# Fewer groups of narrow matmuls in a token-and-channel mixer: hidden product and last query transposes in one PSUM bank, stores at other ticks, second weights through ScalarE

## The chip, the cores and the metric

The kernel runs on one core of one Trainium2 chip. The metric is the device time in microseconds (us) of one execution; the median of three runs stands for a kernel. The engines are named as the profile names them: PE (TensorE matmul) with its weight loads PEld, DVE (VectorE), ACT (ScalarE), POOL (GpSimd) and SP (SyncE, which here only issues transfers).

## The reference, cut to what matters

```
q, k, v: (8 batches, 8 heads, 576 tokens, 64)
q_s = exp(q - max_d q) / (sum_d + 1e-9)            # over the head dimension
k_s = exp(k - max_s k) / (sum_s + 1e-9)            # over the tokens
x   = q_s @ (k_s^T @ v)                            # linear attention, then (8, 576, 512)
u   = x + (relu(x^T @ w_tok1) @ w_tok2)^T          # token mixing, 576 -> 256 -> 576
y   = u + relu(u @ w_ch1) @ w_ch2                  # channel mixing, 512 -> 1536 -> 512
z   = layernorm(y) * g_ln
out = y + relu(z @ w2_ch1) @ w2_ch2                # second channel mixing, 512 -> 2048 -> 512
```

The four channel and two token weights arrive as 64-bit floats and are turned into 32-bit ones on the chip.

## The kernel before

Every product is split into three: each operand is kept as a high and a low part (`hi`, `lo`), and `PASSES` runs hi*hi, hi*lo and lo*hi into the same PSUM bank. So each large product is made of matmuls of 128x128 weights with 512 columns ("wide" below), and PE has little else to do.

There are three stretches. From 0 to about 130 us the first 8 of 32 attention units run alone with the loads of the first weights. One unit is one batch and two heads (class `Unit`). Then come nine blocks of 512 tokens of the first channel mixing (`Phase1`, j = 0 to 8; block 0 is cut in two around block 1, and block 8 is made of the 64 last tokens of each batch), each of 12 steps f. While blocks 0 and 2 to 6 run, the other 24 units run between their wide matmuls, four to a block. From about 868 us on there are nine blocks of the second channel mixing (`Phase2`), 16 steps each.

The order is written out by hand (`tc.manual_schedule`). A clock of ticks moves on in the middle and at the end of each step's two products (`L1`, `L2`), so in `Phase1` one tick is six wide matmuls and a block has 48 ticks; in `Phase2` a tick is a whole product of 12. `later(n, fn)` puts a piece of work n ticks ahead. The units of a block start 10 ticks apart, and `Unit.start` gives each of a unit's pieces its tick (`when`). So the pieces of two units interleave. In a unit's own ticks: 2 transpose of the key maxima (`k_top`, tile pt), 4 its broadcast (`k_sub`, pb), 8 keys times values (pk), 10 the first token product (`tok1`, pg), 11 four query transposes (`q_T(0)`, pq), 12 the fifth (`q_T(1)`, pq), 13 the hidden layer of the token mixing (`hidden`, ph, two fp32 matmuls which the trace shows as four), 15 and 16 the two halves of the second token product (`tok2`, pu). Tick 12 of a unit is tick 2 of the next.

All these narrow pieces take their PSUM bank from one pool of two banks (`ps_att`), in turn: a piece must wait until the piece two before it has been read out. Reading out is a copy of the high part on ACT and a subtraction on DVE for the low part (`split`, `relu_split`).

When a `Phase1` block ends (`finish`, two steps into the next block), DVE adds the residual into yT, POOL adds its low part over all of yT, and four `y_store` pieces follow at ticks 5, 7, 9 and 11 from there: four transposes on PE (py), a copy on ACT and a transfer to `y_dram`.

The weights of the second channel mixing are turned into 32-bit parts in 32 chunks during `Phase1` blocks 7 and 8 and `Phase2` block 0 (class `Loads`, function `decode` with `late` true): a transfer of 512 KB into one of two buffers st, four DVE instructions, a DVE cast for the high part and a POOL subtraction for the low part. `Loads` was given depth 1, so one chunk is fetched ahead. Loads, and the reads of y for the layer norm (`load_y`), all go through SP's queue in program order. `Norm` makes the layer norm of a block: load, statistics, scaling (`hat`), and four groups of transposes (`turn`, px).

Of the kernel before, what the change touches and what calls it, by code (L numbers as in the profile page):

```python
# [16 lines left out]
P = 128  # L17
# [7 lines left out]
def kernel(  # L25
# [61 lines left out]
    def decode(st, w, hi, lo):  # L87
# [38 lines left out]
        def parts():  # L126
            x = w((box["t"] if late else w0).bitcast(F32))
            if late:
                vec.tensor_copy(out=hi, in_=x)  # L129
                nc.gpsimd.tensor_tensor(out=lo, in0=x, in1=hi.bitcast(F32), op=ALU.subtract)  # L130
            else:
                split(x, hi, lo, nc.gpsimd)
# [268 lines left out]
    class Unit:  # L401
# [7 lines left out]
        def start(self, at):  # L409
            steps = (  # L410
                self.k_max, self.k_top, self.q_max, self.q_sub, self.k_sub, self.q_exp,
                self.q_norm, self.k_exp, self.q_split, self.kv, self.tok1,
                lambda: self.q_T(0), self.hidden, lambda: self.q_T(1),
                lambda: self.tok2(0), lambda: self.tok2(1),
            )
            if self.n == 0:
                later(at + 10, lambda: loads.until(3))
                later(at + 14, lambda: loads.until(len(tok)))
            if self.early:
                when = (0, 1, 1, 1, 3, 3, 4, 5, 7, 8, 10, 10, 11, 12, 14, 15)  # L420
            else:
                when = (0, 2, 1, 2, 4, 4, 5, 6, 8, 8, 10, 11, 13, 12, 15, 16)
            for n, fn in zip(when, steps):
                later(at + n, fn)
# [120 lines left out]
        def q_T(self, i):  # L545
# [5 lines left out]
            if not self.early:  # L551
                pq = psum("pq")
                for c in range(c0, c1):
                    m = (c - c0) * P
                    nc.tensor.transpose(out=pq[:, m:m + P], in_=self.qt[:, c], identity=ident)
                split(pq[:, 0:n], self.qT[:, 0, sl], self.qT[:, 1, sl], nc.vector)
# [17 lines left out]
        def hidden(self):  # L574
            ph = psum("ph", self.early)
# [71 lines left out]
    class Phase1:  # L647
# [51 lines left out]
        def finish(self):  # L699
# [14 lines left out]
            if self.f0 == 0:  # L714
                nc.gpsimd.tensor_tensor(out=yT, in0=yT, in1=u[:, 1].bitcast(F32), op=ALU.add)  # L715
            for c in range(CT):
                later(5 + 2 * c, lambda c=c: y_store(self.j, c))
# [10 lines left out]
    class Norm:  # L728
# [3 lines left out]
        def start(self, at):  # L732
# [9 lines left out]
            for kk in range(KD):  # L742
                later(at + 12 + kk + kk // 2, call(self.turn, kk))
# [102 lines left out]
    with tc.manual_schedule():  # L846
# [89 lines left out]
        for o, f in steps:  # L936
            if isinstance(o, Phase1):
# [4 lines left out]
                if f == 0:  # L942
# [3 lines left out]
                    elif o.j == B - 1:  # L946
# [4 lines left out]
                        extra.clear()  # L951
# [6 lines left out]
                        ], 1, 1, 8)  # L958
                        for n in range(5, 29):
                            later(n, lambda: loads.pump(2))  # L960
                        later(10, load_ends)
                    elif o.j == NB - 1:
                        Norm(0).start(18)
# [53 lines left out]
```

## Time and profile before

| | |
|---|---|
| median of 3 runs | 1693.29 us (1693.03 to 1695.51) |
| profiled execution | 1692.61 us, of which the span in the trace is 1690.8 us |
| busy share of the span | PE 98%, PEld 82%, DVE 39%, ACT 23%, POOL 19% |
| wide matmuls | 6048 of PE's 8136 matmuls, 128x512 |
| granted TensorE clock | 0.998 of full speed over the span |

The page's first part gives busy time by engine, its fourth the chain that ended last, followed back from the end; its fifth the groups of instructions. In the timeline view a row is a run of like instructions: start in us from the span's start, length, engine, line, operation, tile written and tiles read, shape and count. Matmuls overlap their neighbours, so the length of a run says less than the distance from its start to the start of the next run; the text below works with these distances.

### The profile page before, as it was taken

The numbers are of one execution on the slowest core, as the hardware profiler recorded it, in microseconds if no ns is written. First come the engines' busy times: TensorE is split into PE (matmuls) and PEld (weight loads), VectorE is DVE, ScalarE is ACT, GpSimd is POOL, SyncE is SP. The second block draws the span as 40 slices with busy tenths as digits, with TensorE's granted clock in tenths as the row PEclk, the third lists the DMA queues.
The fourth block names the chain that finished last, engine by engine and source line by source line (L and its number), as shares of the span: only waits on it lengthen the run. The fifth ranks groups of instructions, "written<-read, shape, count | busy, mean of one in ns | idle before, by whom it ended". The sixth has DMA issues, their size and how long they took to land.

```text
span 1690.8 us, 20156 instructions
## 1 busy us (share of the span) xinstructions
PE 1650.4 (98%) x8136; PEld 1379.6 (82%) x8136; DVE 665.7 (39%) x1322; ACT 393.8 (23%) x792; POOL 314.2 (19%) x220
## 2 busy tenths in 40 slices
PE   5999999999999999999999899999999999999998
PEld 4888888888888888888788788888888888888887
DVE  6875434343433434354567722222213122222211
ACT  4663323333232323311211111111111111111110
POOL 5744522232222313221222200000000000000000
PEclk9999999999999999999999999999999999999999
DMA  8452312122121212042225310101010102010010
GB/s 228 124 169 67 98 33 74 43 56 50 38 67 30 71 38 74 21 144 63 88 63 174 100 51 25 50 25 50 25 51 25 50 1 75 1 53 23 0 50 25
DMA packets 122062, 105.39 MB, mean 62 GB/s; under 512 B 92976, under 2 KB 101424, under 8 KB 118512
## 3 DMA queue, kind: packets, MB, share of 16 engines
q1 hardware_dynamic: 115568, 86.27, 17.6%
q10 hardware_dynamic: 5248, 9.44, 1.6%
q0 software_dynamic: 1152, 8.39, 1.2%
q8 instruction: 64, 1.05, 0.3%
q14 instruction: 30, 0.25, 0.0%
HBM read 82.05 MB, written 22.02 MB: 62 GB/s over the span
## 4 chain that ended last, share of the span: by engine, by line
PE 57%; DVE 3%; DMA 1%; POOL 0%; issue 0%; ACT 0%; SPq 0%; ACTq 0%; DVEq 0%
PE ph L814 22%; PE acc L829 22%; PE acc L692 5%; PE ph L675 5%; PE px L789 1%; DMA st<-in_moe_w_ch 1%; PE pu L592 1%; PE py L622 0%; PE pg L538 0%; DVE t L115 0%; DVE t L121 0%; POOL yT L715 0%; DVE t L108 0%; DMA y<-y_dram 0%; DVE y L778 0%; DMA y_dram<-yn 0%
## 5 line engine op out<-in xcount | busy, mean ns | idle before, releaser
L142 DVE SCALAR_TENSOR_TENSOR h<-ph,h 128x512 fp32r<-128x512 f32 x252 | 174.1, 691 | 687.9 <-ACT h L141 687.8
L814 PE MATMUL ph<-xT,w 128*128 128x512 f32 x1728 | 420.9, 392 | 2.3 <-DVE h L142 1.0
L829 PE MATMUL acc<-w,h 128*128 128x512 f32 x1728 | 420.0, 392 | 0.0
L814 PEld LDWEIGHTS ph<-xT,w 128*128 128x128 f32 x1728 | 322.8, 188 | 73.8 <-DVE h L142 1.6
L829 PEld LDWEIGHTS acc<-w,h 128*128 128x128 f32 x1728 | 323.0, 188 | 68.8
L141 ACT ACTIVATE h<-ph 128x512 fp32r<-128x512 f32 x252 | 150.8, 598 | 858.7 <-PE ph L814 636.3
L692 PE MATMUL acc<-h,w 128*128 128x512 f32 x1296 | 328.7, 396 | 0.0
L675 PE MATMUL ph<-u,w 128*128 128x512 f32 x1296 | 327.7, 396 | 0.0
L675 PEld LDWEIGHTS ph<-u,w 128*128 128x128 f32 x1296 | 236.2, 189 | 46.9 <-DVE u L612 0.4
L692 PEld LDWEIGHTS acc<-h,w 128*128 128x128 f32 x1296 | 236.2, 188 | 45.6
L844 POOL DMA_DIRECT2D out<-y x8 | 4.5, 558 | 637.4 <-DVE y L840 637.4
L467 POOL TENSOR_TENSOR qt<-rawq,qm 128x640 f32<-128x640 f32 x24 | 30.3, 1262 | 235.0 <-PE pt L461 153.7
L538 PE MATMUL pg<-w,qn 128*128 128x256 f32 x480 | 64.8, 286 | 6.4 <-ACT w L137 3.4
L538 PEld LDWEIGHTS pg<-w,qn 128*128 128x128 f32 x480 | 62.2, 193 | 9.8 <-POOL qn L138 3.9
L130 POOL TENSOR_TENSOR w<-t,w 128x512 fp32r<-128x512 f32 x32 | 42.9, 1341 | 130.8 <-DVE w L129 126.3
L592 PE MATMUL pu<-w,hs 128*128 128x288 f32 x384 | 61.4, 295 | 0.0
L592 PEld LDWEIGHTS pu<-w,hs 128*128 128x128 f32 x384 | 54.4, 188 | 0.3 <-ACT hs L141 0.2
L715 POOL TENSOR_TENSOR yT<-yT,u 128x2048 f32<-128x2048 f32 x8 | 37.2, 4648 | 69.8 <-DVE yT L713 65.6
L138 DVE TENSOR_TENSOR qT<-pq,qT 128x512 fp32r<-128x512 f32 (+1 forms) x48 | 21.8, 454 | 71.3 <-ACT qT L137 71.3
L482 POOL TENSOR_TENSOR kt<-rawk,kb 128x640 f32<-128x640 f32 x24 | 37.8, 1575 | 50.2 <-ACT kb L478 50.2
L138 POOL TENSOR_TENSOR qn<-qt,qn 128x640 fp32r<-128x640 f32 x24 | 38.2, 1591 | 41.7 <-ACT qn L137 41.7
L138 DVE TENSOR_TENSOR u<-pu,u 128x288 fp32r<-128x288 f32 x32 | 14.6, 455 | 67.8 <-ACT u L137 67.7
(132 smaller groups left out, 1256.3 us busy)
## 6 DMA issues: line engine op xcount, KB each, us to landing
st<-in_moe_w_ch SPq DMA_DIRECT2D x41, 512.0 KB, 3.7
y<-y_dram SPq DMA_DIRECT2D x18, 1024.0 KB, 4.8
vt<-in_v SPq DMA_DIRECT2D x64, 128.0 KB, 2.9
y_dram<-yn ACTq DMA_DIRECT2D x32, 256.0 KB, 2.4
out<-y POOLq DMA_DIRECT2D x8, 1024.0 KB, 4.1
rawk<-in_k SPq DMA_DIRECT2D x54, 128.0 KB, 2.7
rawq<-in_q SPq DMA_DIRECT2D x27, 256.0 KB, 3.0
stages<-in_moe_w_ch SPq DMA_DIRECT2D x9, 512.0 KB, 4.5
```

The lines of the kernel that those rows point to most:

```text
L130: nc.gpsimd.tensor_tensor(out=lo, in0=x, in1=hi.bitcast(F32), op=ALU.subtract)
L138: engine.tensor_tensor(out=lo, in0=x, in1=hi.bitcast(F32), op=ALU.subtract)
L141: nc.scalar.activation(out=hi, in_=x, func=AF.Relu)
L142: nc.vector.scalar_tensor_tensor(out=lo, in0=x, scalar=0.0, in1=hi.bitcast(F32), op0=ALU.max, op1=ALU.subtract)
L482: nc.gpsimd.tensor_tensor(out=self.kt, in0=self.kr, in1=kb.to_broadcast([P, NC + 1, 2, D]), op=ALU.subtract,)
L538: nc.tensor.matmul(out=pg[:, 0:T], lhsT=self.qn[:, x, c], rhs=w1[:, y, c, :], start=(n == 0), stop=(n == len(terms) - 1),)
L592: nc.tensor.matmul(out=pu[:, 0:HN], lhsT=l, rhs=r, start=(n == 0), stop=(n == len(terms) - 1))
L675: nc.tensor.matmul(out=ps, lhsT=w[:, x, kk, fo:fo + P], rhs=u[:, y, kk], start=(n == 0), stop=(n == 3 * KD - 1),)
L692: nc.tensor.matmul(out=self.acc[dd], lhsT=w[:, x, f % 2, dd * P:(dd + 1) * P], rhs=h[:, y], start=(f == self.f0 and n == 0), stop=(f == se ...
L715: nc.gpsimd.tensor_tensor(out=yT, in0=yT, in1=u[:, 1].bitcast(F32), op=ALU.add)
L814: nc.tensor.matmul(out=ps, lhsT=w[:, x, kk, fo:fo + P], rhs=xT[:, y, kk], start=(n == 0), stop=(n == 3 * KD - 1),)
L829: nc.tensor.matmul(out=self.acc[c], lhsT=h[:, x, c * P:(c + 1) * P], rhs=w[:, y, f % 2], start=(f == 0 and n == 0), stop=(f == self.f1 - 1 ...
```

## The change

It has five parts.

- `hidden` of the 24 late units is moved from tick 13 to tick 12 and into the bank of the fifth query transpose: `q_T(1)` puts its transpose behind column 256 and `hidden` fills columns 0 to 255 of the same tile pq.
- The four stores of blocks 0 to 6 come at ticks 5, 8, 12 and 15 after the block's end (before: 5, 7, 9, 11).
- POOL's addition into yT is cut into four quarters (one per store), two ticks apart from block 2 on.
- The high part of the second weights is copied on ACT in place of DVE.
- The second weights get a third buffer (`stage3`) and depth 2; the load of block 8's input moves from tick 10 to tick 20 (`load_ends`), and the transposes of the first layer norm come three ticks later (15 in place of 12).

```diff
--- before
+++ after
@@ decode
-                vec.tensor_copy(out=hi, in_=x)
+                nc.scalar.activation(out=hi, in_=x, func=AF.Copy)
@@ Unit.start
-                when = (0, 2, 1, 2, 4, 4, 5, 6, 8, 8, 10, 11, 13, 12, 15, 16)
+                when = (0, 2, 1, 2, 4, 4, 5, 6, 8, 8, 10, 11, 12, 12, 15, 16)
@@ q_T
                 pq = psum("pq")
+                if i == 0:
+                    m0 = 0
+                else:
+                    m0 = T
                 for c in range(c0, c1):
-                    m = (c - c0) * P
+                    m = (c - c0) * P + m0
                     nc.tensor.transpose(out=pq[:, m:m + P], in_=self.qt[:, c], identity=ident)
-                split(pq[:, 0:n], self.qT[:, 0, sl], self.qT[:, 1, sl], nc.vector)
+                if i:
+                    self.hidden(pq)
+                split(pq[:, m0:m0 + n], self.qT[:, 0, sl], self.qT[:, 1, sl], nc.vector)
@@ hidden
-        def hidden(self):
-            ph = psum("ph", self.early)
+        def hidden(self, ph=None):
+            if ph is None:
+                if not self.early:
+                    return
+                ph = psum("ph", True)
@@ Phase1.finish
-            if self.f0 == 0:
-                nc.gpsimd.tensor_tensor(out=yT, in0=yT, in1=u[:, 1].bitcast(F32), op=ALU.add)
+            def add(c):
+                x = slice(c * P, (c + 1) * P)
+                nc.gpsimd.tensor_tensor(
+                    out=yT[:, :, x], in0=yT[:, :, x], in1=u[:, 1, :, x].bitcast(F32), op=ALU.add
+                )
+
             for c in range(CT):
-                later(5 + 2 * c, lambda c=c: y_store(self.j, c))
+                if self.f0 == 0:
+                    later(2 * c if self.j > 1 else 0, lambda c=c: add(c))
+                later((5, 8, 12, 15)[c] if self.j < B - 1 else 5 + 2 * c, lambda c=c: y_store(self.j, c))
@@ Norm.start
-        def start(self, at):
+        def start(self, at, turns=12):
-                later(at + 12 + kk + kk // 2, call(self.turn, kk))
+                later(at + turns + kk + kk // 2, call(self.turn, kk))
@@ block 7 starts
-                        extra.clear()
+                        bufs[:] = [w2pool.tile([P, 512, 2], U32, name="stage3")]
+                        extra[:] = [-1, -1, 0]
-                        ], 1, 1, 8)
+                        ], 1, 2, 8)
-                        later(10, load_ends)
+                        later(20, load_ends)
@@ block 8 starts
-                        Norm(0).start(18)
+                        Norm(0).start(18, 15)
```

What stands in a row on an engine changes at three places. First PE, where a unit's `q_T(1)` (pq, L555 before, L559 after) meets the next unit's `k_top` (pt) at the time of a store (py). L675 and L692 (L684 and L701 after) are the wide matmuls, ph<-kvn,gs is `hidden`. Before:

```order
L555 MATMUL pq<-ident,qt 128x128
L461 MATMUL pt<-ident,kmx 128x128
L692 MATMUL acc_4251<-h,w 128x512 x3
L692 MATMUL acc_4252<-h,w 128x512 x3
L577 MATMUL ph<-kvn,gs 128x128 x2
L622 MATMUL py<-ident,yT 128x128 x4
L692 MATMUL acc_4253<-h,w 128x512 x3
L692 MATMUL acc_4254<-h,w 128x512 x3
L474 MATMUL pb<-ident,kmd 128x128
```

After, the same place:

```order
L559 MATMUL pq<-ident,qt 128x128
L586 MATMUL pq<-kvn,gs 128x128 x2
L461 MATMUL pt<-ident,kmx 128x128
L701 MATMUL acc_4246<-h,w 128x512 x3
L701 MATMUL acc_4247<-h,w 128x512 x3
L701 MATMUL acc_4248<-h,w 128x512 x3
L701 MATMUL acc_4249<-h,w 128x512 x3
L474 MATMUL pb<-ident,kmd 128x128
L631 MATMUL py<-ident,yT 128x128 x4
```

`hidden` now stands between the query transpose and pt, and the store behind pb. From the first wide matmul on, the runs of narrow matmuls between wide ones fall from 251 to 222.

The second place is ACT at the same tick, with what each instruction waits for. Before (hs is the evaluated hidden layer, qT 128x64 the fifth query transpose):

```order
L137 ACTIVATE qT<-pq 128x64 [waits PE_49]
L632 ACTIVATE yn<-py 128x512 [waits DMAHW6_49,PE_49]
L635 DMA y_dram<-yn 128x512 [waits DMAHW0_49,Activation_49]
L141 ACTIVATE h<-ph_2045 128x512 [waits PE_49]
L141 ACTIVATE hs<-ph 128x256 [waits PE_49]
```

After, the same unit:

```order
L641 ACTIVATE yn<-py 128x512 [waits PE_49]
L644 DMA y_dram<-yn 128x512 [waits DMAHW7_49,Activation_49]
L141 ACTIVATE hs<-pq 128x256 [waits PE_49]
L137 ACTIVATE qT<-pq 128x64 [waits DVE_49]
L141 ACTIVATE h<-ph_2047 128x512 [waits PE_49]
```

The copy of the fifth transpose now stands behind hs and waits for DVE, where it waited for PE.

The third place is POOL two steps into a block with units: yT is the block's result, qn the low part that `tok1` needs, qt and kt the units' softmax. Before:

```order
L502 TENSOR_TENSOR qt<-qt,qs 128x640
L715 TENSOR_TENSOR yT<-yT,u 128x2048
L138 TENSOR_TENSOR qn<-qt,qn 128x640
L467 TENSOR_TENSOR qt<-rawq,qm 128x640
L482 TENSOR_TENSOR kt<-rawk,kb 128x640
```

After:

```order
L502 TENSOR_TENSOR qt<-qt,qs 128x640
L725 TENSOR_TENSOR yT<-yT,u 128x4x128
L138 TENSOR_TENSOR qn<-qt,qn 128x640
L725 TENSOR_TENSOR yT<-yT,u 128x4x128 x2
L467 TENSOR_TENSOR qt<-rawq,qm 128x640
L725 TENSOR_TENSOR yT<-yT,u 128x4x128
L482 TENSOR_TENSOR kt<-rawk,kb 128x640
```

One quarter of the addition is left ahead of qn. On SP the y load of the second layer norm (L725 before, L740 after) stands behind one more chunk of weights than before.

## Rows read from the trace of the kernel before

**Rows 1.** Waits of PE: releaser, us in total, times, longest us

```profile
PE pg L538 <- POOL qn L138: 3.1, 4, 0.8
```

**Rows 2.** Waits of PEld, columns as above

```profile
PEld pt L461 <- DVE qT L138: 4.6, 13, 0.5
```

**Rows 3.** Timeline of PE, 458 to 491 us, block 3 with its units

```profile
458.85 1.34 PE L538 MATMUL pg<-w,qn 128*128 128x256 f32 x10
...
461.65 1.55 PE L675 MATMUL ph<-u,w 128*128 128x512 f32 x6
...
463.83 1.64 PE L675 MATMUL ph<-u,w 128*128 128x512 f32 x6
...
465.45 1.63 PE L692 MATMUL acc<-h,w 128*128 128x512 f32 x6
...
467.92 1.63 PE L692 MATMUL acc<-h,w 128*128 128x512 f32 x6
...
482.14 1.93 PE L538 MATMUL pg<-w,qn 128*128 128x256 f32 x15
483.90 1.55 PE L692 MATMUL acc<-h,w 128*128 128x512 f32 x6
...
485.64 1.64 PE L692 MATMUL acc<-h,w 128*128 128x512 f32 x6
...
487.36 0.33 PE L461 MATMUL pt<-ident,kmx 128*128 128x128 f32 x1
487.45 1.64 PE L675 MATMUL ph<-u,w 128*128 128x512 f32 x6
...
489.29 1.63 PE L675 MATMUL ph<-u,w 128*128 128x512 f32 x6
...
490.78 1.64 PE L692 MATMUL acc<-h,w 128*128 128x512 f32 x6
```

**Rows 4.** Timeline of POOL in the same block

```profile
454.71 4.59 POOL L715 TENSOR_TENSOR yT<-yT,u 128x2048 f32<-128x2048 f32 x1 [1.01 <-DVE yT L713]
```

**Rows 5.** Timeline of PE in blocks 7 and 8 and in the first block of Phase2

```profile
746.81 0.66 PE L622 MATMUL py<-ident,yT 128*128 128x128 f32 x4 [0.85 <-POOL yT L715]
...
839.06 1.52 PE L692 MATMUL acc<-h,w 128*128 128x512 f32 x6
...
843.38 1.63 PE L692 MATMUL acc<-h,w 128*128 128x512 f32 x6
...
931.60 3.02 PE L814 MATMUL ph<-xT,w 128*128 128x512 f32 x12 [0.96 <-DVE h L142]
...
937.17 2.88 PE L814 MATMUL ph<-xT,w 128*128 128x512 f32 x12
...
943.09 3.01 PE L829 MATMUL acc<-w,h 128*128 128x512 f32 x12
...
952.20 1.63 PE L814 MATMUL ph<-xT,w 128*128 128x512 f32 x6
...
956.92 0.60 PE L789 MATMUL px<-ident,y 128*128 128x128 f32 x4
```

**Rows 6.** Timeline of DVE where it decodes the second weights

```profile
742.35 4.69 DVE L129 CAST w<-t 128x512 fp32r<-128x512 f32 x1
...
912.29 0.42 DVE L129 CAST w<-t 128x512 fp32r<-128x512 f32 x1
921.37 0.43 DVE L100 TENSOR_SCALAR st<-st 128x512 f32<-128x512 f32 x1 [8.67 <-DMA st<-in_moe_w_ch]
...
924.16 0.68 DVE L142 SCALAR_TENSOR_TENSOR h<-ph,h 128x512 fp32r<-128x512 f32 x1
```

**Rows 7.** Groups of instructions, shapes apart: busy us, mean ns, idle before

```profile
L130 POOL TENSOR_TENSOR w<-t,w 128x512 fp32r<-128x512 f32 x32 | 42.9, 1341 | 130.8 <-DVE w L129 126.3 <-PE acc L692 4.5
...
L142 DVE SCALAR_TENSOR_TENSOR hs<-ph,hs 128x256 fp32r<-128x256 f32 x32 | 13.5, 421 | 30.1 <-ACT hs L141 30.1
...
L141 ACT ACTIVATE hs<-ph 128x256 fp32r<-128x256 f32 x32 | 12.4, 386 | 37.3 <-PE ph L577 37.1
```

## The prediction

> **What bounds the kernel now.** PE is busy for 98% of the span (the table above), so the time is PE's work plus PE's stops, and the change leaves its work as it is: the same matmuls, the same shapes. I read the waits of PE and of PEld first, for who stops it, and then the timeline around each, since a run's distance to the next also shows stops that the wait view books elsewhere. The wait of `tok1` for POOL is there four times [rows 1], that of pt's weight load for DVE thirteen times [rows 2]. Each is small; what is to be seen is that they repeat in every block.
>
> A scale is needed. A run of six wide matmuls and four transposes takes 1.74 us (483.90 to 485.64), the same with eight transposes 2.18 (461.65 to 463.83) [rows 3]: a further transpose costs 0.11. Six wide with a single one take 1.49 (489.29 to 490.78) [rows 3], so six wide take 1.38, which is also one tick of `Phase1`.
>
> **The groups themselves.** 29 runs of narrow matmuls are joined to others. Four transposes that join a group cost 0.44, four that stand alone 1.74 - 1.38 = 0.36 [rows 3]. By these rows a group has no price of its own. I take 0; the upper bound is the whole 0.11 of a lone transpose, 29 x 0.11 = 3.2 us. What can be won lies in the waits.
>
> **Hidden layer ahead of pt.** From 485.64 to 487.45 there are six wide matmuls and two transposes, 1.81 us where 1.38 + 0.22 = 1.60 are due [rows 3]: pt stands still 0.21 us, since its bank is still being read by DVE (the first four query transposes). In the changed order `hidden` stands between; alone it takes 1.84 - 1.38 = 0.46 us (487.45 to 489.29) [rows 3], more than the 0.21, so the bank is free when pt comes. 13 x 0.21 = **2.7 us**. The order has 18 such places, so it may be up to 3.8; with nothing won, 0.
>
> **Stores off the hidden layer.** With a store behind it the hidden group takes 2.47 (465.45 to 467.92), against 1.84 + 0.44 = 2.28 [rows 3]. The 0.19 is again a wait for banks, in five blocks: **1.0 us**. The stores now follow pb, pk and the first query transposes, two ticks or more behind the piece whose bank they take.
>
> **The addition into yT in quarters.** `tok1` with its wait takes 2.80 (458.85 to 461.65), without it 1.76 (482.14 to 483.90) [rows 3]. The 1.04 comes from POOL: the addition of 4.59 us [rows 4] stands ahead of qn. A POOL subtraction of 512 columns takes 1.34 [rows 7], so a quarter of the addition does too, and qn comes 4.59 - 1.34 = 3.25 us earlier, three times the wait. Nothing else is late there: the first ten matmuls of `tok1` run before the wait [rows 3]. 4 x 1.04 = **4.2 us**. The other quarters cost POOL 4 x 1.34 - 4.59 = 0.8 us more per block; POOL is busy 19% of the time, and only in block 0, where all four stay together ahead of a unit's kt, may some of the 0.8 reach PE. The store of block 6 waits 0.85 for the same addition [rows 5]. There the first chunk's POOL subtraction now stands ahead: 1.34 + 1.34 in place of 4.59, less what ACT's copy adds; I count **0.8 us**.
>
> **First layer norm three ticks later.** From 839.06 to 843.38 there are six wide matmuls and four transposes, 4.32 us [rows 5] where 1.38 + 0.44 = 1.82 are due: 2.5 us for the scaled y. Three ticks are 4.1 us, more than that, and DVE's work up to there has lost its casts. What comes next, the first `Phase2` step, lies over ten ticks behind. **2.5 us**.
>
> **Second weights.** In the first `Phase2` block PE loses 0.96 us at 931.60, then 5.92 - 2.76 - 0.44 = 2.72 (937.17 to 943.09), then 4.72 - 2.76 = 1.96 (952.20 to 956.92) [rows 5], 5.6 us in all. Each is a matter of DVE being late, and the cause is one row: DVE sits 8.67 us until a chunk lands [rows 6], because its transfer stands in SP's queue behind a y load that waits for the last store. With depth 2 and a third buffer that chunk is issued before the y load. It takes 2.8 us (921.37 to 924.16) [rows 6] inside the idle time, so DVE is 2.8 ahead behind it. Six more chunks follow before the last of the three waits, each without the cast of 0.42 [rows 6]: 2.5 more. The first two waits need 0.96 and 3.7 of lead and get it; the last needs 5.6, since PE comes 3.7 earlier, and gets 5.3. ACT's copy, in order with its other work, may come later than the cast did; I leave 1.2 us standing and count **4.4 us**. Bounds: 1.0, where only the first wait goes, and 5.6.
>
> **Sum.** 2.7 + 1.0 + 4.2 + 0.8 + 2.5 + 4.4 = 15.6 us. The profiled execution took 1692.6 us (span 1690.8 and 1.8 around it): 1677.0. The median of the runs lies 0.7 above the profiled one: **1677.7 us**.
>
> **Rivals.**
>
> *Casts saved, time not.* While POOL added into yT, a cast of DVE took 4.69 us in place of 0.42 [rows 6]: DVE stands still beside POOL. Each chunk's POOL subtraction of 1.34 [rows 7] falls beside the next chunk's DVE instructions, and will after the change. If these then stand still for as much as the cast had cost, the 2.5 us from the casts are lost, the last wait of the weights stays, and the time is 1680.2. For it: the pairing of the two engines stays. Against it: the cast is gone from DVE's queue in any case. The Trainium skill (SBUF — State Buffer, "Who interferes with whom") says that DVE instructions in a two-port mode or with two SBUF inputs and POOL instructions lock each other out for a whole instruction, and that ACT never waits. By that rule, with which the row of 4.69 us agrees, the copy on ACT is free of POOL, but the chunk's other DVE instructions are not, which is this rival.
>
> *The groups have a price.* If a lone transpose's 0.11 is all switching, 29 groups give 3.2 more: 1674.5. Against it stands the 0.36 for four.
>
> *The change doesn't do what it says.* The groups are fewer, but the waits move: two banks serve all the narrow work, and a store behind pb or beside the first query transposes takes a bank out of turn. If the 2.7 and the 1.0 stay, 1681.4. For it: every present wait of this kind is such a collision. Against: the pieces that share a bank are now two ticks (2.8 us) apart.
>
> *Slower: one bank, read in turn.* Hidden layer and fifth transpose now lie in one bank, and ACT's copy of the transpose waits for DVE (the order of ACT above). The chain is ACT 0.39, DVE 0.42 [rows 7], then a smaller ACT copy and a smaller DVE subtraction, at most the same again: 1.6 us, and behind it, on DVE, the maximum that pb waits for. Cover: 12 wide matmuls, 2.76 us, so some 1.1 us to spare. Where DVE or ACT have other work queued ahead and the chain grows by more than 1.1 us, PE stops at every pb, 24 times; each 0.1 us beyond costs 2.4 us. From 0.65 us beyond, all gains are eaten; with 0.8 us the time is 1677.7 + 19.2 = 1697. For it: DVE has an h to read out in the same ticks. Against: pb comes without a wait today, 1.49 us with its six wide matmuls [rows 3]. The Trainium skill (PSUM — Partial Sum Buffer, "Terms") counts two engines on the same bank and partitions at once as a collision, reads against reads included. By that rule the wait on DVE cannot be had without; no run here shows a collision.
>
> **How the numbers follow.** Forecast 0.63; casts saved in vain 0.17; groups with a price 0.05; waits that move 0.07; the bank read in turn 0.08, of which 0.05 within 0.2% of before and 0.03 above. Low end: the forecast with the weights' 1.2 us, pt's 1.1 and the groups' 3.2 in full, 1672.2, rounded to 1672. High end: the waits that move, with the weights at their lower bound (3.4 less), 1684.8, rounded to 1685. About 0.2% (3.4 us) is what a measurement of this kernel can tell from no change, so faster is below 1689.9: 0.92; same 0.05; slower 0.03.
>
> **What would show it.** Right: pt's weight load no longer waits for DVE; no wait of `tok1` for POOL and runs of 1.76 in every block; the first px group without a gap; DVE's 8.67 us before a chunk cut to 6 or less, and PE's three stops in the first `Phase2` block down to about 1 us. Wrong: a new line of pb, py or pq in the waits of PE with some 20 entries; an ACT h that waits behind the copies of the weights; or a run of six wide with one transpose longer than 1.49.

## The result and the profile after

| | before | after |
|---|---|---|
| median of the runs | 1693.69 us (1693.03 to 1695.51, 4 runs) | 1673.78 us (1673.57 to 1674.51, 4 runs) |
| span of the profiled execution | 1690.8 us | 1671.8 us |
| from the first L1 matmul to the end of the span | 1596.5 us | 1577.6 us |

The ratio is 0.9882, with a 95% interval of 0.9864 to 0.9899: 19.9 us less, where the forecast was 15.6 less than the 1693.29 us known then (1677.7 us). The time lies in the forecast's range, but 3.9 us below the forecast itself, so some term was too small, and the experiments look for it.

The third line of the table is the measure used below. It leaves out the start phase, which waits for the first loads and whose length differs by up to 1.8 us between executions, whatever the kernel (the first L1 matmul begins at 94.16 us in one run below and at 95.93 in another). By this line the changed kernel is 18.9 us shorter.

By the first part of its profile page PE still runs 8136 matmuls and is busy for 98% of the span, and the copies have gone from DVE to ACT (DVE runs 1290 instructions where it ran 1322, ACT 824 where it ran 792).

All that is left of the waits of PE in the changed kernel from 100 us on (engine, line and releaser: us in total, times, longest):

```profile
PE pk L514 <- ACT kt L495: 0.6, 1, 0.6
```

The wait of pg for POOL [rows 1] is gone, and in the list of PEld that of pt's weight load for the query transposes on DVE [rows 2]. The wait of pk was there before, but shorter. This line and one of PEld that is gone too, in the kernel before:

```profile
PE pk L514 <- ACT kt L495: 0.2, 1, 0.2
...
PEld ph L577 <- DVE qT L138: 2.7, 10, 0.4
```

The second line is the hidden layer: its weight loads waited too, at five places with two loads each. The prediction doesn't name this line; it becomes important below.

The block of [rows 3], on PE in the changed kernel (start, length, engine, line, operation, count):

```profile
454.83 1.93 PE L538 MATMUL pg<-w,qn 128*128 128x256 f32 x15
456.60 1.55 PE L684 MATMUL ph<-u,w 128*128 128x512 f32 x6
...
472.16 1.28 PE L514 MATMUL pk<-vt,kt 128*128 128x130 f32 x10
...
476.49 1.93 PE L538 MATMUL pg<-w,qn 128*128 128x256 f32 x15
...
480.44 1.62 PE L701 MATMUL acc<-h,w 128*128 128x512 f32 x6
481.90 0.27 PE L559 MATMUL pq<-ident,qt 128*128 128x128 f32 x1
482.01 0.61 PE L586 MATMUL pq<-kvn,gs 128*128 128x128 f32 x4
482.45 0.27 PE L461 MATMUL pt<-ident,kmx 128*128 128x128 f32 x1
482.48 3.02 PE L684 MATMUL ph<-u,w 128*128 128x512 f32 x12
```

`tok1` takes 1.77 us (454.83 to 456.60) where it took 2.80 [rows 3]. From 480.44 to 482.48 stand six wide matmuls, one transpose, the hidden layer and pt, 2.04 us. Due are 1.38 + 0.11 + 0.44 + 0.11 = 2.04 (the hidden layer's 0.44 is 482.01 to 482.45): pt doesn't wait.

POOL at that place, in the changed kernel (in brackets the idle time before, and what ended it):

```profile
450.75 1.27 POOL L725 TENSOR_TENSOR yT<-yT,u 128x512 f32<-128x512 f32 x1 [1.01 <-DVE yT L722]
```

A quarter of 1.27 us stands ahead of qn, which begins at 452.52, in place of 4.59 [rows 4].

The first layer norm and the first `Phase2` block on PE, in the changed kernel:

```profile
834.35 0.60 PE L804 MATMUL px<-ident,y 128*128 128x128 f32 x4
...
836.18 0.60 PE L804 MATMUL px<-ident,y 128*128 128x128 f32 x4
...
925.77 0.60 PE L804 MATMUL px<-ident,y 128*128 128x128 f32 x4
...
928.97 0.60 PE L804 MATMUL px<-ident,y 128*128 128x128 f32 x4
```

834.35 to 836.18 is 1.83 us where [rows 5] showed 4.32, and the stops of the first `Phase2` block [rows 5] are gone altogether: 12 wide matmuls and four transposes take 3.20 (925.77 to 928.97).

Why, is seen on DVE (the first two lines) and in SP's queue (the others), in the changed kernel:

```profile
899.53 0.42 DVE L100 TENSOR_SCALAR stage<-stage 128x512 f32<-128x512 f32 x1
...
908.85 1.29 DVE L768 BATCH_NORM_STATS2 st<-y 128x6 f32<-128x512 f32 x2 [3.33 <-DMA y<-y_dram]
...
889.45 0.34 SPq L183 DMA_DIRECT2D stage<-in_moe_w_ch  x1
902.99 0.33 SPq L740 DMA_DIRECT2D y<-y_dram  x1
```

One more chunk is issued ahead of the y load: of the 32, 24 stand there in SP's queue (the last at 889.45), and 23 stood there in the kernel before. DVE works on this chunk from 899.53 on, in what was idle time, and its 8.67 us of idleness [rows 6] have become 3.33. They now end with y itself, not with a chunk.

One place is worse, block 1. PE (first line) and POOL there, in the changed kernel:

```profile
190.29 1.39 PE L514 MATMUL pk<-vt,kt 128*128 128x130 f32 x10 [0.60 <-ACT kt L495]
...
182.92 5.02 POOL L725 TENSOR_TENSOR yT<-yT,u 128x512 f32<-128x512 f32 x4 [0.97 <-DVE yT L722]
```

The four quarters stand together ahead of kt (187.90), and pk loses 0.85 us (by the distances of its run) where it lost 0.41 before.

### The profile page after: what moved, and what is told of

It is laid out like the page before. It is cut to its first block, busy times and chain, and to the rows that moved or that the text cites. A ratio compares the mean times of both kernels' runs of the same rounds, so it can differ in the third digit from the quotient of the medians.

```text
span 1671.8 us, 20195 instructions
## 1 busy us (share of the span) xinstructions
PE 1642.0 (98%) x8136; PEld 1380.9 (83%) x8136; DVE 644.3 (39%) x1290; ACT 410.1 (25%) x824; POOL 318.5 (19%) x244
## 4 chain that ended last, share of the span: by engine, by line
PE 94%; DVE 2%; POOL 1%; issue 1%; ACT 1%; DMA 1%; SPq 0%; POOLq 0%; DVEq 0%; ACTq 0%
PE ph L829 24%; PE acc L844 24%; PE ph L684 17%; PE acc L701 17%; PE pu L601 4%; PE pg L538 3%; PE pk L514 2%; PE py L631 1%; PE px L804 1%; PE pq L559 1%; PE pq L586 1%; DMA rawq<-in_q 0%; DVE spare L138 0%; DVE dt L108 0%; POOL yT L725 0%
## 5 line engine op out<-in xcount | busy, mean ns | idle before, releaser
L684 PE MATMUL ph<-u,w 128*128 128x512 f32 x1296 | 324.7, 395 | 0.0
L701 PE MATMUL acc<-h,w 128*128 128x512 f32 x1296 | 323.7, 394 | 0.0
L701 PEld LDWEIGHTS acc<-h,w 128*128 128x128 f32 x1296 | 237.1, 188 | 46.7
L684 PEld LDWEIGHTS ph<-u,w 128*128 128x128 f32 x1296 | 236.8, 188 | 46.7 <-DVE u L621 0.4
L725 POOL TENSOR_TENSOR yT<-yT,u 128x512 f32<-128x512 f32 x32 | 43.0, 1359 | 37.9 <-DVE yT L722 37.9
L129 ACT ACTIVATE w<-t 128x512 fp32r<-128x512 f32 x32 | 20.3, 633 | 97.0 <-DVE t L121 94.6
```

The lines of the kernel that those rows point to most:

```text
L684: nc.tensor.matmul(out=ps, lhsT=w[:, x, kk, fo:fo + P], rhs=u[:, y, kk], start=(n == 0), stop=(n == 3 * KD - 1),)
L701: nc.tensor.matmul(out=self.acc[dd], lhsT=w[:, x, f % 2, dd * P:(dd + 1) * P], rhs=h[:, y], start=(f == self.f0 and n == 0), stop=(f == se ...
L725: nc.gpsimd.tensor_tensor(out=yT[:, :, x], in0=yT[:, :, x], in1=u[:, 1, :, x].bitcast(F32), op=ALU.add)
```

## The experiments

Each is the changed kernel with the edit that is shown. "Main phase" is the time from the first L1 matmul to the end of the span, and the last column is its distance to the changed kernel's 1577.6.

| run | span | first L1 | main phase | against after | median |
|---|---|---|---|---|---|
| after_again | 1672.1 | 94.36 | 1577.8 | +0.2 | 1673.88 |
| hidden_alone | 1675.1 | 94.39 | 1580.7 | +3.1 | 1676.80 |
| hidden_own_bank | 1694.0 | 95.05 | 1599.0 | +21.4 | 1695.88 |
| stores_alone | 1676.6 | 94.94 | 1581.7 | +4.1 | 1677.73 |
| whole_add | 1679.8 | 95.40 | 1584.4 | +6.8 | 1680.77 |
| turns_12 | 1675.5 | 95.93 | 1579.6 | +2.0 | 1677.01 |
| cast_on_dve | 1675.4 | 95.36 | 1580.0 | +2.4 | 1676.99 |
| depth_one | 1678.5 | 94.75 | 1583.8 | +6.1 | 1679.93 |
| weights_as_before | 1680.3 | 94.28 | 1586.0 | +8.4 | 1681.91 |
| weights_all_before | 1689.1 | 94.19 | 1594.9 | +17.3 | 1691.17 |
| reload_10 | 1674.7 | 94.68 | 1580.0 | +2.4 | 1676.56 |
| two_quarters_dve | 1671.6 | 95.11 | 1576.4 | -1.2 | 1673.30 |

**The scale.** `after_again` is the changed kernel once more. (The first figures of its expectation are a slip for 1673 to 1675.)

> The changed kernel itself, beside the runs of the same call. 1573 to 1575 us... as measured before: 1673.8 us, and 1577.6 us from the first L1 matmul to the end of the span, within 0.5.

It agrees within 0.2 us. The main phase of each run below is that of one profiled execution; on the strength of this one pair, differences of half a microsecond and more are read as real. The medians, which hold the start phase, move with them within 1.3 us.

**The hidden layer behind the fifth transpose again**, with a bank and a tick of its own.

```diff
-                when = (0, 2, 1, 2, 4, 4, 5, 6, 8, 8, 10, 11, 12, 12, 15, 16)
+                when = (0, 2, 1, 2, 4, 4, 5, 6, 8, 8, 10, 11, 13, 12, 15, 16)
...
-                if i:
-                    self.hidden(pq)
...
-                ph = psum("ph", True)
+                ph = psum("ph", self.early)
```

> The changed kernel with one thing undone: the hidden layer is at its own tick 13 in a bank of its own again, behind the fifth query transpose (the stores keep their new ticks). Times from the first L1 matmul to the end of the span, 1577.6 us in the changed kernel. Theory of the prediction: pt's weight load waits for DVE again, 13 places or more of 0.2, +2.6, and 24 more groups of narrow matmuls cost nothing of their own: 1580.2 us. Rival one (a group has a price, about 0.04 us as the remainder of the result would have it): 1.0 more, 1581.2 us. Rival two (a group costs a whole lone transpose, 0.11): 2.6 more, 1582.8 us. Rival three (two banks' order, not the place of the hidden layer, made pt wait, and the stores' new ticks already mend it): no wait of pt, 1577.6 to 1578.6 us.

Measured: +3.1 us. The waits of PEld for DVE's reading of the query transposes, in this run from 100 us on:

```profile
PEld ph L579 <- DVE qT L138: 2.7, 10, 0.4
PEld pt L461 <- DVE qT L138: 2.6, 7, 0.5
```

pt waits again, at 7 places where it waited at 13 [rows 2], and the hidden layer waits just as in the kernel before (2.7, 10, 0.4), though no store stands behind it any more. So the 1.0 us that the prediction gave to the stores belongs to the same cause as the 2.7: two banks in turn, of which one is still being read. Moving the stores changes at which piece the turn falls badly: it ends six of pt's thirteen waits and none of the hidden layer's. Rival three holds for those six places and falls for the rest.

The 3.1 us are a balance. pk in block 1 and DVE's additions ahead of it, in this run, and below them the additions in the changed kernel:

```profile
190.16 1.28 PE L514 MATMUL pk<-vt,kt 128*128 128x130 f32 x10
...
179.72 2.48 DVE L715 TENSOR_TENSOR yT<-acc,u 128x512 f32<-128x512 f32 x4
...
180.37 2.48 DVE L722 TENSOR_TENSOR yT<-acc,u 128x512 f32<-128x512 f32 x4
```

pk doesn't wait here, and gives back the 0.85 us, so some 3.9 us are lost among the units. This is more than the 2.6 of the expectation, since the hidden layer's waits were not in it; between no price of a group and a small one the sum can't tell. It also shows what made pk worse in the changed kernel: there DVE reads out the hidden layer ahead of its additions into yT, they begin 0.65 us later, and with them POOL's quarters and kt, while PE, which has not stopped for pt, has its six wide matmuls ahead of pk 0.63 us sooner (188.17 for 188.80).

**The price of a group by itself.** The stores go to ticks where mostly nothing else stands.

```diff
-                later((5, 8, 12, 15)[c] if self.j < B - 1 else 5 + 2 * c, lambda c=c: y_store(self.j, c))
+                later((7, 11, 13, 17)[c] if self.j < B - 1 else 5 + 2 * c, lambda c=c: y_store(self.j, c))
```

> The changed kernel with its stores at ticks 7, 11, 13 and 17 behind a block's end in place of 5, 8, 12 and 15: mostly ticks without other narrow work, so 20 more groups and nothing else added. It measures the price of a group by itself. Times from the first L1 matmul to the end of the span, 1577.6 us in the changed kernel, less the waits that a store may meet at its new place (read from the trace). Theory of the prediction, no price: 1577.6 us. Rival one, 0.04 us each as the remainder of the result would have it: +0.8, 1578.4 us. Rival two, 0.11 us each: +2.2, 1579.8 us.

Measured: +4.1 us, but not for the groups. Two stores of a block in this run's timeline on PE, the second alone in the middle of twelve wide matmuls, the first with a wait:

```profile
463.07 1.62 PE L701 MATMUL acc<-h,w 128*128 128x512 f32 x6
465.00 0.63 PE L631 MATMUL py<-ident,yT 128*128 128x128 f32 x4 [0.31 <-DVE qT L138]
...
475.31 1.28 PE L514 MATMUL pk<-vt,kt 128*128 128x130 f32 x10
...
477.81 0.60 PE L631 MATMUL py<-ident,yT 128*128 128x128 f32 x4
...
479.62 1.94 PE L538 MATMUL pg<-w,qn 128*128 128x256 f32 x15
```

From pk to pg, with the store alone: 479.62 - 475.31 = 4.31 us. The same work with the store joined to pk, in the changed kernel above: 476.49 - 472.16 = 4.33. A group has no price. The 4.1 us are waits: six wide matmuls ahead of the first store take 465.00 - 463.07 = 1.93 in place of 1.46, since pt stands right ahead and the store takes the bank that DVE reads. One such store of 0.50 us and one of 0.25 in each of five blocks make 3.8, by the distances in the trace.

**The hidden layer at its new place, but in its own bank.**

```diff
-                pq = psum("pq")
-                if i == 0:
-                    m0 = 0
-                else:
-                    m0 = T
+                if i:
+                    self.hidden(psum("ph"))
+                pq = psum("pq")
+                m0 = 0
...
-                if i:
-                    self.hidden(pq)
```

> The changed kernel with the hidden layer at the same place, ahead of the fifth query transpose and pt, but in a bank of its own in place of the half of that transpose's bank. Theory (two banks taken in turn; what counts is whose bank is still being read): pt now takes the bank of the hidden layer just written, and must wait for ACT's 0.39 and DVE's 0.42 on it, 0.7 to 1.2 us in each of 18 places: 1577.6 + 13 to 22 = 1591 to 1600 us from the first L1 matmul to the end of the span. Rival (the bank that is read in turn by ACT and DVE for two owners is what costs; a bank each is better or the same): 1577.6 us within 0.5, or less.

Measured: +21.4 us, slower than the kernel before. The wait of PE in this run from 100 us on that makes it:

```profile
PE pt L461 <- DVE hs L142: 18.5, 18, 1.2
```

Three banks are now asked for in one group where two exist, so pt waits until the hidden layer has been read out. What makes the merge pay is the shared bank; the place alone would have lost it all. The Trainium skill (PSUM — Partial Sum Buffer, "Terms") counts a read of ACT beside a read of DVE in one bank and the same partitions as a collision; the program keeps the two apart by waits, no run here shows one, and the prediction's slower rival, which took those waits for the danger, fell: with the bank shared no wait of pb is to be seen.

**POOL's addition undivided.**

```diff
-                if self.f0 == 0:
-                    later(2 * c if self.j > 1 else 0, lambda c=c: add(c))
+            if self.f0 == 0:
+                nc.gpsimd.tensor_tensor(out=yT, in0=yT, in1=u[:, 1].bitcast(F32), op=ALU.add)
```

> The changed kernel with one thing undone: POOL's addition into yT is one instruction again, issued when the block ends (the stores keep their new ticks). Times are from the first L1 matmul to the end of the span, 1577.6 us in the changed kernel, since the start phase differs by up to 1.8 us between executions. Theory of the prediction: tok1 waits for qn again in four blocks, 4 x 1.04 = 4.2, and the first store of block 6 again 0.85; pk's wait in block 1 shrinks from 0.85 to about 0.4. Sum +4.6: 1582.2 us. Rival (the new ticks of the stores, not the quarters, took tok1's wait away): 1577.6 within 0.5 and no wait of pg for POOL.

Measured: +6.8 us. The waits of PE in this run from 100 us on:

```profile
PE pg L538 <- POOL qn L138: 3.3, 4, 0.8
PE pk L514 <- ACT kt L495: 1.5, 1, 1.5
PE py L631 <- POOL yT L730: 0.9, 1, 0.9
```

By the distances, `tok1` loses 4 x 1.09, the store of block 6 another 1.0 and the transposes of the layer norm in the first `Phase2` block 0.5. The step on pk was wrong in sign: it loses 1.70, not 0.4. So the quarters are not what made pk worse in the changed kernel; with the addition whole it would have been worse still. What did is shown by `hidden_alone` above.

**The first layer norm's transposes at tick 12.**

```diff
-                        Norm(0).start(18, 15)
+                        Norm(0).start(18, 12)
```

> The changed kernel with one thing undone: the transposes of the first layer norm begin at tick 12 again, not 15. Theory of the prediction: the three ticks are what hides the wait for the scaled y; 2.5 us come back in one stop of px, 1673.8 + 2.5 = 1676.3 us. Rival (DVE reaches the scaled y earlier because the casts of the weights have left it, so most of the wait would have gone without the three ticks): a stop of 1 us or less, at most 1674.8 us.

Measured: +2.0 us, in one stop, on PE in this run:

```profile
833.94 0.78 PE L804 MATMUL px<-ident,y 128*128 128x128 f32 x2 [1.08 <-DVE y L793]
```

The stop is 2.1 us by the distances, against 2.6 in the kernel before: most of the term is the three ticks' own, and the rival, at most 1 us, falls. The half microsecond may be the absent casts; no run tells.

**The second weights, piece by piece.** First the cast on DVE again, then the buffers, then both.

```diff
-                nc.scalar.activation(out=hi, in_=x, func=AF.Copy)
+                vec.tensor_copy(out=hi, in_=x)
```

> The changed kernel with one thing undone: the copy of each chunk's high half is a cast on DVE again (the third buffer and depth 2 stay). Theory of the prediction: DVE's early chunk gives 2.8 us of lead and the absent casts the rest, of 5.6 us needed by the last stop in the first Phase2 block. Without the casts 2.8 us of PE's stops come back there: 1673.8 + 2.8 = 1676.6 us, and the wait of px or L2 for DVE is to be seen again near 950. Rival (the casts were saved in vain; the early chunk alone does it): no stop comes back, 1673.8 us within 0.5, and the first Phase2 block is as in the changed kernel.

Measured: +2.4 us. In this run's timeline PE stops again at the third place of the kernel before (there 952.20 to 956.92 [rows 5], some 15 us later in the span, with the same two waits), and not near 950 as expected:

```profile
939.27 0.73 PE L829 MATMUL ph<-xT,w 128*128 128x512 f32 x2 [0.59 <-DVE w L129]
940.73 1.19 PE L829 MATMUL ph<-xT,w 128*128 128x512 f32 x4 [0.73 <-POOL w L130]
```

The casts were not saved in vain.

```diff
-                        bufs[:] = [w2pool.tile([P, 512, 2], U32, name="stage3")]
-                        extra[:] = [-1, -1, 0]
+                        extra.clear()
-                        ], 1, 2, 8)
+                        ], 1, 1, 8)
```

> The changed kernel with one thing undone: two buffers and depth 1 for the second weights, as before (the copy stays on ACT, the reload of the ends stays at tick 20). Theory of the prediction: the chunk is again issued behind the y load, DVE stands some 8 us until it lands, and of the 5.6 us of PE's stops the absent casts save 2.5: 1673.8 + 3.1 = 1676.9 us. Rival one (the order of the transfers doesn't matter once the casts are off DVE): 1673.8 us within 0.5. Rival two (the whole gain was the early chunk, the casts gave nothing): 1673.8 + 5.6 = 1679.4 us.

Measured: +6.1 us, twice the 3.1 expected. DVE and PE at the first stop in this run's timeline:

```profile
910.71 0.43 DVE L100 TENSOR_SCALAR st<-st 128x512 f32<-128x512 f32 x1 [10.45 <-DMA st<-in_moe_w_ch]
...
915.40 4.60 PE L829 MATMUL ph<-xT,w 128*128 128x512 f32 x12 [2.44 <-DVE h L142]
919.85 2.88 PE L844 MATMUL acc<-w,h 128*128 128x512 f32 x12
```

The stretch behind the stop in the windows view of this run (length, busy time of PE, PEld, DVE, ACT and POOL, granted clock of PE as a share of full speed, DMA share, GB/s):

```profile
915.30:919.30 4.00, 3.90 (x10) 3.07 (x11) 3.83 (x10) 0.21 (x1) 0.18 (x1) 0.57 0.29 108
```

The chunk lands 7.1 us after its issue between the two y loads (5.7 in the kernel before), DVE stands 10.45 us, and PE's first stop is 2.44 us in place of 0.96 [rows 5]. Behind the stop the granted clock is 0.57: twelve wide matmuls take 919.85 - 915.40 = 4.45 us in place of 2.72. That is 1.7 us more which no term of mine had. Why the chunk lands later isn't settled; what the trace shows is that 0.5 MB and the two y loads of 1 MB each then share transfer engines that are busy for 0.89 of the time from 903.5 to 910.7 us (0.82 at that place in the kernel before).

> The changed kernel with both undone: two buffers and depth 1, and the cast on DVE; the reload of the ends alone stays at tick 20. Every theory in which the second weights' 5.6 to 5.8 us come from these two expects them back: 1673.8 + 5.7 = 1679.5 us, with PE's three stops near 931, 940 and 954 again. If the later reload of the ends was what mattered, 1673.8 us. What it tells beside the two runs in which one alone is undone: whether their costs add up to this one (2.8 + 3.1 by the prediction) or whether either alone is enough (then both of those stay near 1673.8 and this one doesn't).

Measured: +8.4 us. The first stop on PE in this run:

```profile
914.93 4.39 PE L829 MATMUL ph<-xT,w 128*128 128x512 f32 x12 [2.53 <-DVE h L142]
```

The window behind the stop, in this run:

```profile
915.30:919.30 4.00, 4.00 (x13) 3.17 (x13) 3.79 (x10) 0.00 (x0) 0.43 (x2) 0.67 0.32 121
```

The stop is as long as with depth 1 alone, and the clock falls again, to 0.67. 2.4 + 6.1 = 8.5 against 8.4: the two parts add up, and neither stands in for the other.

**The reload of the ends.** The last piece, tick 20 in place of 10, had no term in the prediction. It is undone first on top of `weights_as_before` (`weights_all_before`), then alone (`reload_10`).

```diff
-                        later(20, load_ends)
+                        later(10, load_ends)
```

> The changed kernel with all of its second weights undone: two buffers, depth 1, cast on DVE, and the reload of the ends at tick 10 again. The run that kept the reload at tick 20 lost 8.4 us where the kernel before loses 5.7, with a first stop of 2.5 us in place of 0.96. If the reload's place made the difference: 1577.6 + 5.7 = 1583.3 us and a first stop of about 1 us. If it did not, and the landing of the chunk between the two y loads decides (8.4 us from its issue in that run, 5.7 in the kernel before): again about 1586.0 us, a first stop of 2 us or more and slow matmuls behind it. From the first L1 matmul to the end of the span.

Measured: +17.3 us, 8.9 more than with the reload at 20, and neither expectation came near. The rows of POOL, SP, DVE and PE at the place in this run's timeline:

```profile
745.87 1.29 POOL L725 TENSOR_TENSOR yT<-yT,u 128x512 f32<-128x512 f32 x1
...
747.18 0.34 SPq L652 DMA_DIRECT2D u<-u_dram  x1
...
757.53 0.43 DVE L100 TENSOR_SCALAR st<-st 128x512 f32<-128x512 f32 x1 [13.08 <-DMA st<-in_moe_w_ch]
...
761.06 5.49 PE L684 MATMUL ph<-u,w 128*128 128x512 f32 x12 [7.29 <-DVE h L142]
```

The window behind the stop, in this run:

```profile
761.00:767.00 6.00, 5.94 (x14) 4.69 (x15) 5.74 (x10) 0.41 (x1) 2.10 (x2) 0.51 0.53 175
```

The reload overwrites the u that POOL's fourth quarter still reads. The whole addition ended 5 us after it began; the last quarter ends at 747.16, and SP stands until then (its next issue is at 747.18) with the chunks behind it. DVE waits 13.08 us for a chunk, an h that PE needs stands behind that chunk in DVE's queue, and PE stops 7.29 us, with the clock at half behind it. That place loses 10.3 us, the first `Phase2` block most of the other 7.

> The changed kernel with one thing undone: the reload of the ends at tick 10 again (third buffer, depth 2 and ACT's copy stay). The reload overwrites the u that the fourth quarter of the addition still reads, until about 747, and in SP's queue the chunks of the second weights stand behind it. Theory one (it blocks SP whatever the depth): DVE waits for a chunk for some 10 us and PE stops about 7 us near 761, as in the run with all second weights undone: 1577.6 + 7 to 10 = 1585 to 1588 us from the first L1 matmul to the end of the span. Theory two (depth 2 has issued two chunks by 743 and so covers the delay of some 4 us until 747): no stop of PE, 1577.6 us within 0.5; then the reload's place is needed only with depth 1.

With depth 2 and ACT's copy the same reload costs 2.4 us: SP stands as long, but one more chunk has been issued ahead of the reload (four, where it was three). PE's one stop there in this run:

```profile
761.88 3.01 PE L684 MATMUL ph<-u,w 128*128 128x512 f32 x12 [2.17 <-DVE h L142]
```

The window behind the stop, in this run:

```profile
761.90:766.00 4.10, 4.10 (x18) 3.41 (x19) 3.89 (x6) 1.72 (x3) 1.30 (x1) 1.00 0.48 142
```

Both theories were wrong in size: depth 2 covers most of the delay, not all.

**A better version.** In block 1 DVE adds two of the quarters, and block 6 stores a tick later.

```diff
+                engine = nc.vector if self.j == 1 and c < 2 else nc.gpsimd
-                nc.gpsimd.tensor_tensor(
+                engine.tensor_tensor(
-                later((5, 8, 12, 15)[c] if self.j < B - 1 else 5 + 2 * c, lambda c=c: y_store(self.j, c))
+                later((6 if self.j == B - 2 else 5, 8, 12, 15)[c] if self.j < B - 1 else 5 + 2 * c, lambda c=c: y_store(self.j, c))
```

> A version meant to be better than the changed kernel: in block 1, where the four quarters of POOL's addition stand together ahead of kt and pk waits 0.85 us, DVE adds two of the quarters; and the first store of block 6 comes a tick later (0.15 us of wait today). Theory: POOL's part falls from 5.0 to 2.5 us, kt and pk come in time: 0.85 + 0.15 less, 1576.6 us from the first L1 matmul to the end of the span. Rival (DVE and POOL lock each other out, so DVE's two quarters stand in POOL's way as long as they last, or DVE's h comes late): between 1577.1 and 1578.5 us.

Measured: 1576.4 us in the main phase, 1.2 and 1.3 less than the changed kernel's two executions; no wait of PE is left from 100 us on. The medians of the runs, 1673.30 (1672.86 to 1673.87) against 1673.88 (1673.75 to 1674.76), point the same way, but their ratios to the kernel before, 0.9874 (0.9859 to 0.9889) and 0.9878 (0.9864 to 0.9893), overlap: the gain is read from the trace of one execution, not from the times. POOL and DVE in block 1 of this run:

```profile
183.90 3.50 POOL L726 TENSOR_TENSOR yT<-yT,u 128x512 f32<-128x512 f32 x2 [0.97 <-DVE yT L722]
...
183.85 2.39 DVE L726 TENSOR_TENSOR yT<-yT,u 128x512 f32<-128x512 f32 x2
```

Two quarters on POOL alone would be 2.5 (5.02 for four); beside DVE they take 3.50, and DVE's two take 2.39 where four additions of that width, with one input in PSUM, take 2.48 (180.37 above). So each engine stood for part of the time while the other worked, and 1.5 us are won where 2.5 were moved; it was enough. The Trainium skill (SBUF — State Buffer, "Who interferes with whom") says just that: DVE instructions with two SBUF inputs and POOL's that read SBUF lock each other out. These rows agree.

## Why the prediction held, and where it was short

Both kernels run the same 6048 wide matmuls in the same order, so the start of each in the two traces, counted from the first, says what had been gained by then. By places:

| step | predicted | gone in the trace | undone alone |
|---|---|---|---|
| groups themselves | 0 | nothing to assign | 0 (4.31 against 4.33) |
| hidden ahead of pt, stores off it | 2.7 + 1.0 | 4.6 | +3.1, or 3.9 without pk (the hidden layer only) |
| quarters, `tok1` | 4.2 | 4.1 | 4 x 1.09 |
| store of block 6 | 0.8 | 0.9 | 1.0 |
| first layer norm | 2.5 | 2.6 | +2.0 |
| second weights | 4.4 | 6.0 | +8.4, or +17.3 with the reload |
| store of block 1, pk of block 1 | none | 0.9, and -0.4 | |

By the last wide matmul 18.6 us are gone (the terms are rounded); the other 0.3 of the main phase's 18.9 lie behind it.

In the second line the stops of pt and of the hidden layer themselves make 2.6 + 1.0. The other 1.0 lies in the same units, those that stop, and what it is stays open. It is no price of the groups: a unit that stops nowhere is as long before as after. The fourth of a block, from its pg to the pt behind it, takes 446.46 - 427.45 = 19.01 us before, with the hidden layer as a group of its own, and 442.43 - 423.44 = 18.99 after, with it joined to the transpose.

**What was right.** The waits were read from the right rows, and what the prediction said would show them right is in the trace: no wait of pt's weight load for the transposes on DVE, `tok1` in 1.77, the first px group without a gap, no new wait of pb. The groups have no price, as the rows of four transposes, joined and alone [rows 3], had said. The rivals fell one by one: casts saved in vain (`cast_on_dve` loses 2.4), a price of the groups (`stores_alone`), waits that move (only pk's in block 1 did, by 0.4 us; others do where a piece is put badly, as in that run), and the bank read in turn.

**The step that was short: the second weights.** One chunk passes the y load, as predicted, and its mechanism is right. What was mis-sized is the reserve: 1.2 us were left standing in case ACT's copy came late. It doesn't where it counts. PE's last stop waits for chunk 30 of the 32, for its low part on POOL, here in the kernel before and, below, in the changed one:

```profile
954.44 1.39 POOL L130 TENSOR_TENSOR w<-t,w 128x512 fp32r<-128x512 f32 x1 [3.41 <-DVE w L129]
...
935.79 1.29 POOL L130 TENSOR_TENSOR w<-t,w 128x512 fp32r<-128x512 f32 x1 [2.02 <-ACT w L129]
```

It ends at 955.83 and at 937.08, 18.75 us earlier. PE had gained 12.76 us up to that block (counted, like these, from the span's start), so the lead is 6.0 us, where the prediction had 5.3. Before, DVE's cast of this chunk began 1.18 us behind the instruction ahead of it (952.77 to 953.95), since an h stood between; ACT's copy begins 0.04 us behind it. The three stops are 6.0 us by the distances, not 5.6 (the first is 931.60 - 927.75 - 2.72 = 1.13, since the 0.96 is only the wait). So 6.0 were needed, 6.0 are there, and all three stops go: 6.0 - 4.4 = 1.6 us of the 3.3 by which the sum of 15.6 fell short of 18.9. Another 0.9 is the second line of the table (4.6 for 3.7), 0.5 the store of block 1 less pk, which was not in the sum, and 0.3 lies behind the last wide matmul.

**What the sum left out: the reload.** I read it as a detail of the second weights. It is a condition of the quarters: cut in four and spread over six ticks, the addition frees its u later, and the reload of that buffer at tick 10 would have stood in SP's queue ahead of the chunks. In the changed kernel that would have cost 2.4 us, with the old buffers 8.9. As it moved along, the forecast didn't suffer; but nothing in my working had looked.

**What was right by luck.** The prediction gave 2.7 us to the hidden layer's new place and 1.0 to the stores' new ticks. `hidden_alone` shows these two terms made up otherwise: with the stores at their new ticks and no store behind it, the hidden layer still waits in five blocks, so that 1.0 is won by joining it to the transpose; and six of pt's thirteen waits, some 1.2 us at 0.2 each, go by the stores alone. The sizes of the two terms were near, what was put into each was not; the cause of both is the turn of the two banks.

## What to carry to other kernels

With two buffers taken in turn, a wait belongs to the order of takers and not to the piece that shows it: before moving a piece, list who takes the buffer two places ahead and whether it has been read by then, and where three would be taken at one time, let two share. When an instruction is cut up and spread, its last part sets when its inputs come free, so look for what reloads them and what is queued behind that load. To find what a chunk ahead is worth, go to the instruction that PE waits for last and ask when it ends, with what stands ahead of it on each engine; a reserve needs a row that asks for it, too.

## What the runs showed of the hardware

A stop of PE can cost more than itself. Behind stops of 2.44 and 2.53 us (`depth_one`, `weights_as_before`) and of 7.29 us (`weights_all_before`) the granted clock was 0.57, 0.67 and 0.51 over the 4 to 6 us that followed, which is the lower of TensorE's two levels, 1.2 GHz, for most of that time: in `weights_all_before` 14 matmuls took 5.94 us, 0.42 each, in place of 0.227. Behind the stop of 2.17 us in `reload_10` the clock stayed at 1.00, and so it did in the first `Phase2` block of the kernel before, whose stops are shorter.

The length of a stop alone doesn't decide it. In `weights_all_before` PE stops for 1.01 and 0.73 us with two transposes between (939.24 and 940.70), the same pair as in the kernel before (1.03 and 0.72, at 941.08 and 942.55). There the clock stayed at 1.00; here the granted clock is 0.50 from 941 to 943 us, and twelve wide matmuls take 4.27 us (941.28 to 945.55):

```profile
941.28 4.43 PE L844 MATMUL acc<-w,h 128*128 128x512 f32 x12
```

What makes the difference the runs don't show.

The clock is one part of why undoing the second weights costs more (8.4 us in `weights_as_before`) than doing them won (6.0): the first stop is some 1.5 us longer than in the kernel before, the slow matmuls behind it cost another 1.5, and the second stop is 0.7 shorter.
